# The order of the blocks behind a test at a kernel's end: the general path ahead of the empty arm

## The chip, the core and the metric

The kernel runs on one core of a Trainium2 chip. The metric is device time in microseconds (us): from the start of the program on the core to its end, with all inputs and the output in the chip's memory. The profile shows one execution of the same program, instruction by instruction; its span runs from the first recorded instruction to the last.

## What is computed

The reference is an attention block whose scores are masked by a hash, followed by a Fourier mixing block with a two-layer network. Shapes: batch 4, 8 heads, 768 positions, head size 64, so 512 channels; the hidden layer has 2048 channels.

```python
q_bits = (np.einsum('bhsd,dk->bhsk', q, proj) > 0).astype(np.int64)
k_bits = (np.einsum('bhsd,dk->bhsk', k, proj) > 0).astype(np.int64)
...
mask = q_bucket[:, :, :, None] == k_bucket[:, :, None, :]
scores = scale * np.matmul(q, k.transpose(0, 1, 3, 2))
scores = np.where(mask, scores, -1000000000.0)
scores = scores - np.max(scores, axis=-1, keepdims=True)
attn = np.exp(scores)
attn = attn / (np.sum(attn, axis=-1, keepdims=True) + 1e-09)
...
X = np.fft.fft(x, axis=1)
X = np.fft.fft(X, axis=2)
u = x + np.real(X).astype(np.float32)
un = (u - mean(u)) / np.sqrt(var(u) + 1e-06)
return u + np.maximum(un @ w_ch1, 0.0) @ w_ch2
```

## The kernel before, in words

The program has two complete versions of the computation, one behind the other.

**The main path** (`_main`) is the one that these inputs need. It leaves out the subtraction of the row maximum before the exponential, which is allowed while the scores are small, and it reads the weights from eight-byte words by shifting bits, which is allowed while the weights are ordinary numbers. It works through the four batches: the attention of one batch is interleaved with the mixing and the network of the batch before it. Its last work is the network of batch 3, in `outer7`: PE makes products (L1270), VectorE adds them up with scale (L1282, L1316, L1318, L1322), and SyncE (SP) issues the stores of 128 rows to the output (L1024).

While it works, the main path records the largest norms of queries and keys and whether a weight was out of the ordinary. Before the last batch's network it makes a flag `fl` of these (L1536), and `values_load` (L1539) has every one of the five engines load this flag into a register of its own: the variable `large`.

**The general path** (`_any_scores`, L121 to L483) does everything again without these assumptions. It runs only if the flag is set. With these inputs it is not set, so none of its instructions is executed; but they are in the program of each engine, and they take up room there. In the built program the general path has 260 instructions on SP, 842 on ACT, 1760 on DVE, 116 on POOL and 5288 on PE (matmuls and their weight loads together more).

**The test** is in the last lines of the kernel, L1558:

```python
    with tc.If(large > 0, preferred_fallthrough_block=False):
        _any_scores(tc, *args, cn)
```

An engine has one stream of instructions, laid out block by block. The test becomes, on each engine, a conditional branch (CompareAndBranch) and two arms: the true arm, which is the general path, and a false arm without work. The false arm is not wholly empty. Because the general path would have used up and counted on semaphores, the false arm brings the semaphores to a common state: one wait-and-set on ACT, PE, DVE and POOL, and eight of them on SP, one for each DMA semaphore. SP's waits are for the last transfers of the main path. After the arms comes the end of the program (the profile puts it down to L1589), where all engines meet at a barrier and the semaphores are cleared. On SP the end has 14 semaphore instructions and three drains.

The argument `preferred_fallthrough_block` says which arm lies directly behind the conditional branch and is reached by simply going on. With False, as before, the stream of an engine reads:

```
main path | conditional branch | false arm, jump to the end | general path | end
```

So the kernel before goes on from the branch into the false arm and then jumps over the whole general path to the end. Which queue an instruction stands in isn't touched by any of this: output stores are issued by SP, the five engines each test for themselves, and the order within the main path is fixed ahead of the test.

Of the kernel before, what the change touches and what calls it, by code (L numbers as in the profile page):

```python
# [1552 lines left out]
def kernel(tc, *args):  # L1553

    cn = {n: tc.nc.inline_tensor(a, name="k_" + n) for n, a in _consts().items()}
    with ExitStack() as ctx:
        large = _main(ctx, tc, *args, cn)
    with tc.If(large > 0, preferred_fallthrough_block=False):  # L1558
        _any_scores(tc, *args, cn)


# [32 lines left out]
```

## Time and profile before

| what | value |
|---|---|
| median of 3 runs | 1102.72 us (1101.38 to 1104.4) |
| the profiled execution's own time | 1102.7 us |
| its span, first to last instruction | 1100.4 us |
| granted TensorE clock over the span | 0.994 |
| instructions executed | 14144 |
| VectorE busy | 790.5 us (72%) |
| ScalarE busy | 499.5 us (45%) |
| GpSimd busy | 58.6 us (5%) |
| last matmul group (L1270), start and length | 1085.46 us, 5.34 us |
| last store issued by SP (L1024), start and length | 1092.45 us, 0.90 us |

The span is shorter than the execution's own time by 2.3 us, which lie outside the recorded instructions. Names with a q, such as SPq or DVEq, are the sequencer of an engine: it handles branches, semaphores and the issue of DMAs, and none of this counts as busy time. DMA queues q8 and q14 are of the kind "instruction": what they move are the engines' own instruction streams.

### The profile page before, as it was taken

Reading aid. Unit: us, or ns where it says so; the run is one execution under the profiler, and the core shown is the slowest. Engines: PE = TensorE matmul, PEld = TensorE weight load, DVE = VectorE, ACT = ScalarE, POOL = GpSimd, SP = SyncE. Lnnn points to the kernel's source line nnn. Section 1 sums busy time; section 2 is a strip of 40 time slices with the busy share of each in tenths; the row PEclk is TensorE's granted clock in tenths of the full one; section 3 lists DMA queues with packets and bytes.
Section 4 is the critical chain, followed back from the end, with each engine's and each line's share of the span. In section 5 each row is a group of like instructions: output and inputs, shape, how many; then the busy total and the mean of one; then the engine's idle time right before and its main releaser. Section 6 shows DMA issues by size and latency. Waiting matters only on the chain.

```text
span 1100.4 us, 14144 instructions
## 1 busy us (share of the span) xinstructions
PE 1043.3 (95%) x4933; PEld 632.7 (57%) x4933; DVE 790.5 (72%) x1336; ACT 499.5 (45%) x1055; POOL 58.6 (5%) x132
## 2 busy tenths in 40 slices
PE   7989897999989999999999999999999999999996
PEld 3333353446744675545664576645674569768575
DVE  5899958878599977776767785965856785644353
ACT  6987555553276324454326433355315522340420
POOL 0000000002000020010000011001000002100000
PEclk9999999999999999999999999999999999999998
DMA  9755353451056161322154134213032205122301
GB/s 222 224 95 126 64 140 72 138 164 19 20 149 209 44 204 26 68 63 66 26 157 107 48 82 153 44 43 92 15 129 68 68 24 172 55 81 88 123 20 41
DMA packets 175710, 103.13 MB, mean 94 GB/s; under 512 B 129552, under 2 KB 162960, under 8 KB 175632
## 3 DMA queue, kind: packets, MB, share of 16 engines
q1 hardware_dynamic: 169840, 88.65, 30.1%
q0 software_dynamic: 4224, 13.11, 3.7%
q8 instruction: 41, 0.67, 0.2%
q10 hardware_dynamic: 1568, 0.39, 0.2%
q14 instruction: 37, 0.30, 0.1%
HBM read 81.14 MB, written 20.97 MB: 93 GB/s over the span
## 4 chain that ended last, share of the span: by engine, by line
PE 61%; DVE 11%; ACT 4%; DMA 2%; issue 2%; DVEq 0%; SPq 0%; ACTq 0%
PE o L1270 22%; PE h_p L1390 20%; PE oo L914 6%; PE sc L893 6%; DVE pk L903 3%; PE cs L1086 2%; DMA zraw<-in_moe_w_ch_dram 2%; PE A L1115 2%; PE B L1115 1%; DVE acc L988 1%; ACT rr L948 1%; DVE w L1282 1%; DVE h L1256 1%; PE bits L825 1%; PE un L1141 1%
## 5 line engine op out<-in xcount | busy, mean ns | idle before, releaser
L1270 PE MATMUL o<-w,h 128*128 128x256 f32 x1152 | 259.4, 382 | 1.2 <-ACT tq L1289 0.7
L1270 PEld LDWEIGHTS o<-w,h 128*128 128x128 f32 x1152 | 216.3, 190 | 43.6 <-issue 4.6
L897 ACT ACTIVATE pk<-sc 128x768 f32<-128x768 f32 x192 | 147.6, 809 | 78.4 <-PE sc L893 60.9
L1390 PE MATMUL h_p<-x,w 128*128 128x384 f32 x448 | 163.5, 495 | 3.2 <-ACT h L1412 1.5
L893 PE MATMUL sc<-qt,kt 64*128 64x384 f32 x768 | 155.7, 508 | 6.0 <-ACT pk L897 5.7
L914 PE MATMUL oo<-pk,vn 128*64 128x385 f32 (+1 forms) x768 | 155.3, 499 | 6.0 <-DVE pk L903 3.0
L903 DVE SCALAR_TENSOR_TENSOR pk<-qb,kb,pk 128x768 f32<-128x768 bf16 x132 | 129.0, 1012 | 30.2 <-ACT pk L897 30.1
L1390 PEld LDWEIGHTS h_p<-x,w 128*128 128x128 f32 x448 | 82.3, 190 | 71.0 <-ACT pk L897 5.4
L988 DVE TENSOR_TENSOR acc<-acc,pk 128x1536 f32<-128x1536 f32 (+1 forms) x72 | 105.7, 1482 | 7.2 <-ACT pk L897 6.7
L1390 PE MATMUL h_p<-w 128*128 128x384 f32 x288 | 105.5, 489 | 2.3 <-ACT w L1427 2.3
L914 PEld LDWEIGHTS oo<-pk,vn 128*64 128x64 f32 x768 | 49.1, 136 | 100.0 <-issue 69.3
L893 PEld LDWEIGHTS sc<-qt,kt 64*128 64x128 f32 x768 | 66.9, 188 | 51.3 <-issue 24.0
L1390 PEld LDWEIGHTS h_p<-w 128*128 128x128 f32 x288 | 53.7, 190 | 41.7 <-ACT w L1427 3.5
L1300 ACT COPY tq<-o 128x256 f32<-128x256 f32 x24 | 8.9, 372 | 105.1 <-PE o L1270 105.1
L1282 DVE SCALAR_TENSOR_TENSOR w<-o,rs,w 128x256 f32<-128x256 f32 x56 | 26.7, 478 | 41.6 <-PE o L1270 41.6
L1270 PE MATMUL o<-w 128*128 128x256 f32 x176 | 42.3, 383 | 1.3 <-DVE w L1282 1.3
L1416 DVE TENSOR_TENSOR h<-h 128x384 f32<-128x384 f32 x32 | 17.8, 556 | 33.1 <-ACT h L1415 33.1
L1289 ACT COPY tq<-o 128x256 f32<-128x256 f32 x24 | 8.9, 371 | 69.3 <-PE o L1270 69.2
L1270 PEld LDWEIGHTS o<-w 128*128 128x128 f32 x176 | 32.8, 190 | 8.8 <-DVE w L1282 2.9
L1423 DVE TENSOR_TENSOR h<-h 128x384 f32<-128x384 f32 x32 | 17.7, 553 | 27.0 <-ACT h L1422 27.0
L1024 POOL DMA_DIRECT2D out_dram<-w x30 | 16.4, 548 | 388.7 <-issue 293.2
L1086 PE MATMUL cs<-ch,z 128*128 128x128 f32 (+3 forms) x192 | 33.2, 324 | 3.0 <-DVE bt L829 1.9
(170 smaller groups left out, 1312.4 us busy)
## 6 DMA issues: line engine op xcount, KB each, us to landing
w<-ad SPq DMA_DIRECT2D x168, 128.0 KB, 2.0
w<-bd SPq DMA_DIRECT2D x42, 512.0 KB, 4.5
zraw<-in_moe_w_ch_dram POOLq DMA_DIRECT2D x16, 512.0 KB, 4.0
bd<-w SPq DMA_DIRECT2D x14, 512.0 KB, 3.9
vn<-in_v_dram SPq DMA_DIRECT2D x32, 192.0 KB, 3.4
qn<-in_q_dram SPq DMA_DIRECT2D x120, 48.0 KB, 2.4
kn<-in_k_dram SPq DMA_DIRECT2D x60, 96.0 KB, 3.4
zraw<-in_moe_w_ch_dram SPq DMA_DIRECT2D x8, 512.0 KB, 5.7
```

The source lines that it names most:

```text
L893: last[0] = nc.tensor.matmul(ps[:, h, 0:HALF], kt[rows, ks], qt[rows, qs], start=kb is not None, stop=True,)
L897: nc.scalar.activation(pk[:, g, :, 0:HALF], ps[:, :, 0:HALF], AF.Exp, scale=SCALE)
L903: nc.vector.scalar_tensor_tensor(w, qb[:, h].rearrange("p (g s) -> p g s", g=2), kb[:, h, c : c + 1], w, op0=ALU.is_equal, op1=ALU.mult,)
L914: nc.tensor.matmul(oos[g][h * D : (h + 1) * D, 0:w], nat["v", n][:, (2 * c + h) * D : (2 * c + h + 1) * D], pk[:, g, h, 0:w], start=(c == ...
L988: nc.vector.tensor_tensor(acc[:, g], (first if c == 1 else acc)[:, g], new[:, g], op=ALU.add,)
L1086: nc.tensor.matmul(ps[:, pc + 2 * lo : pc + 2 * hi - 1 : 2], z[:, cp, pc, par, t * P : (t + 1) * P], ch[:, cp, pc, lo:hi], start=(cp == 0) ...
L1115: nc.tensor.matmul(ps[:, cols], F[:, par, k, t, j * P : (j + 1) * P], sq[:, t, k, cols], start=(t == 0), stop=(t == 1),)
L1270: nc.tensor.matmul(ps, a[:, r], right7[i][:, r], start=start and r == 0, stop=r == HF // 2 - 1, skip_group_check=not start,)
L1282: nc.vector.scalar_tensor_tensor(t[:, cols], src, r, t[:, cols], op0=ALU.mult, op1=ALU.add)
L1390: nc.tensor.matmul(ps, left[:, k], right[i][:, k], start=start and k == 0, stop=k == 1, skip_group_check=not start,)
L1416: nc.vector.tensor_tensor(c21, c12, c21, op=ALU.add)
L1423: nc.vector.tensor_tensor(c22, c21, c22, op=ALU.add)
```

## The change

One argument is turned over. The general path is laid directly behind the conditional branch; the false arm follows it, and the end of the program follows the false arm.

```diff
-    with tc.If(large > 0, preferred_fallthrough_block=False):
+    with tc.If(large > 0, preferred_fallthrough_block=True):
         _any_scores(tc, *args, cn)
```

The stream of an engine now reads:

```
main path | conditional branch | general path, jump to the end | false arm | end
```

The instructions themselves are the same. On each engine the built program has as many as before (SP: 1103 in both), and the end of the program begins at the same place in it. The conditional branch now has the opposite condition: where the flag isn't set, it jumps to the false arm. The listing of the program still has a jump at the end of the false arm, but its target is the next instruction, and in the assembled program it is gone; the jump that is left is the one at the end of the general path. Everything ahead of the branch stands where it stood.

## The prediction

> **What bounds the kernel now.** I read the head of the page first, then the end of the chain of waits and the timeline of the last 15 us, and then, for the two lines that the change concerns, the instructions of L1558 (the test) and L1589 (the end of the program), the waits of SP, and the instruction queue in short windows.
>
> The head of the page says what the kernel as a whole is bound by:
>
> ```profile
> span 1100.4 us, 14144 instructions
> PE 1043.3 (95%) x4933; PEld 632.7 (57%) x4933; DVE 790.5 (72%) x1336; ACT 499.5 (45%) x1055; POOL 58.6 (5%) x132
> ```
>
> PE is busy for 95% of the span. Nothing of that can move: the instructions ahead of the branch are the same at the same places. What the change can touch is only what comes after each engine's branch. The last steps of the timeline (start us, length us, engine, line) show where that begins:
>
> ```profile
> 1085.46 5.34 PE L1270 MATMUL o<-w,h 128*128 128x256 f32 x24
> ...
> 1091.94 0.48 DVE L1282 SCALAR_TENSOR_TENSOR u<-tq,rs,u 128x256 f32<-128x256 f32 x1
> 1092.45 0.90 SPq L1024 DMA_DIRECT2D out_dram<-u  x1
> ```
>
> The computation ends at 1092.4 and the span at 1100.4: 8.0 us are a tail with no arithmetic in it. The instructions of the test, all engines (count, min/median/max ns, first and last start us):
>
> ```profile
> L1558 SPq EVENT_SEMAPHORE  x8: 17/17/17, 1095.5 to 1096.0; - x8
> L1558 POOLq COMPARE_BRANCH  x2: 38/39/40, 961.2 to 961.4; - x2
> L1558 PEldq COMPARE_BRANCH  x2: 95/1754/3413, 1087.4 to 1091.0; - x2
> L1558 ACTq COMPARE_BRANCH  x2: 38/46/53, 1088.0 to 1088.2; - x2
> L1558 DVEq COMPARE_BRANCH  x2: 51/56/60, 1092.6 to 1092.8; - x2
> L1558 SPq COMPARE_BRANCH  x2: 41/47/53, 1093.4 to 1096.1; - x2
> ```
>
> Each engine executes two branches: the test, and the jump from the false arm over the general path to the end (both bear the same name here). The instructions of the end:
>
> ```profile
> L1589 SPq EVENT_SEMAPHORE  x14: 17/28/28, 1098.7 to 1100.3; - x14
> ...
> L1589 POOLq DRAIN  x3: 40/107/5388, 961.8 to 1100.1; - x3
> ...
> L1589 ACTq DRAIN  x2: 8/44/81, 1090.7 to 1099.8; - x2
> L1589 PEldq DRAIN  x2: 8/40/72, 1094.5 to 1099.9; - x2
> L1589 DVEq DRAIN  x2: 10/34/58, 1095.8 to 1099.8; - x2
> ```
>
> The two views together give the price of the jump. From the start of the second branch to the first instruction of the end: SP 1096.1 to 1098.7, 2.6 us; ACT 1088.2 to 1090.7, 2.5; DVE 1092.8 to 1095.8, 3.0; PE 1091.0 to 1094.5, 3.5; POOL 961.4 to 961.8, only 0.4. POOL's general path has 116 instructions, SP's 260 and the others' more. SP is last at the barrier, by 2.9 us, so its path sets the end. Its waits, in the last 10 us:
>
> ```profile
> SPq L1558 <- SPq L1558: 2.0, 1, 2.0
> ```
>
> SP comes out of the test at 1093.45, sits 2.0 us until the last output store has landed (1095.5), passes its eight semaphores in 0.6 us, and only then jumps, for 2.6 us. The wait and the jump stand one behind the other.
>
> [...] 2.5 to 3.5 us on the four engines with a far target, and 0.4 on POOL with a near one. In the window 1096.9:1098, inside SP's jump, the instruction queue shows one fetch and no other transfer:
>
> ```profile
> DMA packets 1, 0.01 MB, mean 7 GB/s; under 512 B 0, under 2 KB 0, under 8 KB 0
> ...
> q14 instruction: 1, 0.01, 2.8%
> ```
>
> [...] the trace has 41 and 53 ns on SP. The branch as such is free; the fetch is what is paid. [...]
>
> **The change part by part.** (1) The jump moves from behind the false arm to ahead of it. Its number stays one per engine and its length too, within the 8 instructions of SP's arm: over the general path. (2) The second branch goes: 41 ns on SP, with its step under 0.1 us. (3) The false arm and the end lie next to each other, in the order in which they are executed, with no jump between them.
>
> For SP: the conditional branch starts at 1093.4, as before, since it follows the issue of the last store. It is now the far jump. With SP's own 2.6 us it reaches the false arm at 1093.4 + 2.6 = 1096.0. The last store has landed at 1095.5, so the first semaphore is there already: the 2.0 us wait lies wholly beside the jump. Eight semaphores at the same 0.6 us: 1096.6, and the end begins there instead of at 1098.7: 2.1 us saved. The jump's price is the unknown term. Before, SP's fetch ran on an empty chip (above); after, it runs at about 1094.3, beside the last store. The nearest row for that is DVE's jump, whose fetch fell into the window 1093.5:1094.5 among 150 packets of the store:
>
> ```profile
> q1 hardware_dynamic: 150, 0.14, 40.9%
> q14 instruction: 1, 0.01, 3.9%
> ```
>
> It cost 3.0 us. With this, SP reaches the arm at 1096.4, the end at 1097.0, and 1.7 us are saved. Bounds: with PE's 3.5 us the end begins at 1093.4 + 3.5 + 0.6 = 1097.5, 1.2 us saved. With POOL's 0.4 us the landing at 1095.5 is what SP waits for, and the end begins at 1096.1, 2.6 us saved. More than that isn't there to be had, because the landing and the eight semaphores stay. I take 1.8 us, nearer to DVE's case than to the empty one, because the store is sure to be under way.
>
> The other engines: PE's branch is executed at 1087.4, while its matmuls are queued and run until 1090.8; a jump of 3.5 us ends at 1090.9, and PE is at the barrier some 3.4 us earlier, for no gain. It hides under the last matmuls; without that cover it would end where it did. ACT's ends at 1088.0 + 2.5 = 1090.5. DVE's branch at 1092.6 with 3.0 us ends at 1095.6, 0.2 earlier than before. POOL was through at 961.8 but for a drain of its own. So all four still wait for SP, and SP's gain reaches the end in full. From the first instruction of the end to the last of the span are 1.7 us, as before: the same instructions at the same place.
>
> Sum, against the profiled execution: 1100.4 - 1.8 = 1098.6 us of span, and 1102.7 - 1.8 = 1100.9 us of time, with the 2.3 us outside the span as they were. The median of the runs shown, 1102.72, is the profiled execution's time, so nothing is added.
>
> **The rivals.** *The fetch waits behind the store.* [...] If it is served only after the landing at 1095.5, then SP goes on about 1.7 us after that (in its jump before, the fetch was seen from 1096.9 on and SP went on at 1098.7, at most 1.8): 1097.3, plus 0.6, 1097.9, and 0.8 us are saved: 1101.9. For it: two of the last three stores take about 3 us to land. Against it: DVE's fetch got through in the midst of such packets and delayed DVE by 0.5 us against ACT's empty case.
>
> *A second miss: slower.* If the false arm lies on another page than the end, SP jumps into the first and must fetch the second right after it. That puts a second stall of 2.6 to 3.0 us behind the arm: 1096.0 + 0.6 + 2.6 = 1099.2, or 1096.4 + 0.6 + 3.0 = 1100.0, against 1098.7: 0.5 to 1.3 us slower, 1103.2 to 1104.0. It becomes slower than before as soon as the extra stall is over the 1.8 us gained. For it: a fetch in q14 is 8 KB (37 packets, 0.30 MB on the page of the profile[...])[...]. Against it: the end itself, which is at the same place, ran before without a gap (14 semaphores from 1098.7 to 1100.3)[...]. To be slower by over 3.3 us it would have to stall twice more.
>
> *It does nothing.* If another engine came last, or if SP's store and not its jump set the end, the time would stay at 1102.7. That SP comes to the end 2.9 us after DVE speaks against the first, and the second is the upper bound above, where the gain is largest, not nothing.
>
> **How the numbers follow.** The forecast (1.2 to 2.6 us saved) has 0.77, the waiting fetch 0.10, nothing 0.05, the second miss or a stall that the trace doesn't show 0.08. A difference of under 0.3%, which is 3.3 us, is about what a measurement of this kernel can't tell from no change. The forecast, 0.16%, is inside that, and so is its upper bound of 2.6 us (0.24%). The three runs of before lie 3 us apart, so a median may be off by about 1 us: of the forecast's cases I put 0.14 beyond 3.3 us by scatter, and of the others 0.01. So faster 0.15, same 0.79, slower 0.06, the last from the second miss and scatter together. The range is the forecast's 1100.1 to 1101.5 widened by the scatter below, 0.9 us, and above to the cases of no gain with a little scatter: 1099.2 to 1103.0.
>
> **What would show it right or wrong.** In the profile after: one branch per engine in L1558; SP's eight semaphores begin 2.6 to 3.0 us after its branch, at about 1096.0 to 1096.4 where the branch is at 1093.4, and follow each other without waiting; SP's first instruction of the end follows within 0.1 us of the eighth; PE's branch takes about 3.4 us under its last matmuls; the wait of SP's L1558 on itself is gone or a long pause without a releaser. The prediction is wrong if SP's semaphores start only 3.5 us or more after the branch (the fetch waits), if a gap of over 1 us stands between the arm and the end (a second miss), or if anything ahead of the branch takes another time.

## The result and the profile after

The changed kernel took 1098.18 us (median of 7 runs, 1096.92 to 1100.02), the kernel before 1102.72 us in the same comparison (7 runs, 1100.77 to 1104.4). The ratio is 0.9964 with a 95% interval of 0.9951 to 0.9976: 4.5 us less, where 1.8 were forecast. Two later comparisons of the same two programs gave 0.9983 and 0.9986. So the first thing to settle is how much of the 4.5 us belongs to the change.

Its profiled execution took 1099.06 us, with a span of 1097.1 us. The head of the page of the changed kernel:

```profile
span 1097.1 us, 14139 instructions
PE 1044.5 (95%) x4933; PEld 633.2 (58%) x4933; DVE 790.7 (72%) x1336; ACT 499.3 (46%) x1055; POOL 58.4 (5%) x132
```

Five instructions fewer: one branch on each engine. The instructions of the test in the changed kernel (count, min/median/max ns, first and last start us):

```profile
L1558 SPq EVENT_SEMAPHORE  x8: 17/17/17, 1094.9 to 1095.4; - x8
...
L1558 PEldq COMPARE_BRANCH  x1: 3362/3362/3362, 1085.9 to 1085.9; - x1
L1558 ACTq COMPARE_BRANCH  x1: 54/54/54, 1086.6 to 1086.6; - x1
L1558 ACTq EVENT_SEMAPHORE  x1: 17/17/17, 1089.1 to 1089.1; - x1
...
L1558 DVEq COMPARE_BRANCH  x1: 72/72/72, 1091.1 to 1091.1; - x1
L1558 SPq COMPARE_BRANCH  x1: 50/50/50, 1092.0 to 1092.0; - x1
L1558 DVEq EVENT_SEMAPHORE  x1: 21/21/21, 1094.6 to 1094.6; - x1
```

and those of the end, of which one line matters:

```profile
L1589 SPq EVENT_SEMAPHORE  x14: 17/28/28, 1095.5 to 1097.1; - x14
```

SP's two lines are one row in time. SP branches at 1092.0 and comes to its false arm at 1094.9: 2.9 us for the far jump, now ahead of the eight semaphores. The eight follow each other without a wait (1094.9 to 1095.4), and the end begins at once, at 1095.5; before, 2.6 us lay between. In SP's waits of the last 9 us its pause of 2.0 us, which stood ahead of the jump, has become the jump itself:

```profile
SPq L1558 <- SPq L1558: 2.9, 1, 2.9
```

The last store, issued at 1091.54, lands 2.9 us later, at 1094.4. SP comes out of its jump 0.5 us after that, so the landing costs it nothing any more. PE's jump takes 3.4 us under its own last matmuls, ACT's and DVE's are over before SP's.

From SP's branch to the end of the span that makes 5.1 us, where the kernel before took 1100.4 - 1093.4 = 7.0: 1.8 us less to within the rounding, which is the forecast's figure. But SP's branch itself comes 1.4 us earlier than in the profiled execution of before, and nothing that was changed lies ahead of it. The timeline shows where these 1.4 us are from. The same group of eight matmuls, 276 us after the start, first in the kernel before and then in the changed one (start us, length us):

```profile
277.58 1.89 PE L1270 MATMUL o<-w,w 128*128 128x256 f32 x8
```

```profile
276.20 1.89 PE L1270 MATMUL o<-w,w 128*128 128x256 f32 x8
```

and the last 24 matmuls of the changed kernel, which started at 1085.46 before:

```profile
1084.02 5.34 PE L1270 MATMUL o<-w,h 128*128 128x256 f32 x24
```

1.38 us at 276 us, 1.44 us at 1084 us: the lead is there after the first quarter and stays as it is. The profiled pair is thus 3.6 us apart (1102.7 - 1099.06) for three reasons: 1.8 us in the tail, 1.4 us in the first 276 us, and 0.4 us outside the span (2.3 before, 1.9 after). The experiments ask which of these come back.

### The profile page after: what moved, and what is told of

The parts are those of the page before. It is cut to its first block, busy times and chain, and to the rows that moved or that the text cites. A ratio compares the mean times of both kernels' runs of the same rounds, so it can differ in the third digit from the quotient of the medians.

```text
span 1097.1 us, 14139 instructions
## 1 busy us (share of the span) xinstructions
PE 1044.5 (95%) x4933; PEld 633.2 (58%) x4933; DVE 790.7 (72%) x1336; ACT 499.3 (46%) x1055; POOL 58.4 (5%) x132
## 4 chain that ended last, share of the span: by engine, by line
PE 61%; DVE 12%; ACT 4%; issue 2%; DMA 2%; DVEq 0%; SPq 0%; ACTq 0%
PE o L1270 23%; PE h_p L1390 19%; PE oo L914 6%; PE sc L893 6%; DVE pk L903 3%; PE cs L1086 2%; PE A L1115 2%; DMA zraw<-in_moe_w_ch_dram 2%; PE B L1115 1%; DVE acc L988 1%; ACT rr L948 1%; DVE w L1282 1%; DVE h L1256 1%; PE bits L825 1%; PE un L1141 1%
```

## The experiments

Theory A: the change is worth its tail, because the fetch that the far jump needs now runs beside the last store; the rest is scatter. Theory B: the order of the blocks also makes the part ahead of the branch faster. Other rivals stand with the runs. Where an edit adds lines, the test's line moves from L1558 to L1561 or L1563, and the end's from L1589 to L1592 or L1594.

### Both kernels again, and the general path cut short

The first two of these four runs change nothing. The other two cut the general path to a few instructions, which makes the jump's target near; what they leave out is not executed with these inputs.

```diff
     const = ctx.enter_context(tc.tile_pool(name="const_g", bufs=1))
+    off = const.tile([P, 2], F32, tag="off", name="g_off")
+    nc.sync.dma_start(off, cn["off"].ap())
+    nc.vector.tensor_scalar(off, off, 1.0, None, op0=ALU.mult)
+    nc.sync.dma_start(out[0, 0:P, 0:2], off)
+    return
```

> The kernel before, once more, for the scatter. Theory A (the gain is the far jump laid beside the last store, 1.8 us in the span, and some 0.4 us outside the span; the rest of the 4.5 us between the medians is scatter of the work ahead of the branch): SP's conditional branch starts anywhere from 1091 to 1095 us, the tail from it to the end of the span is 7.0 us again, 2.3 us lie outside the span, median 1101.5 to 1103. Theory B (the order of the blocks also makes the work ahead of the branch faster by 1.5 to 2.5 us): the branch starts at 1093.4 or later and the ratio to the kernel before is 1.000.

Measured: 1102.39 us (14 runs), ratio to the kernel before 0.9996 (0.9985 to 1.0006). The profiled execution took 1105.43 us, 1.9 of them outside the span. So the 2.3 us of the first profile aren't the old order's: 0.4 of the 3.6 us were scatter. The instructions of SP's test in this run:

```profile
L1558 SPq EVENT_SEMAPHORE  x8: 17/17/17, 1098.5 to 1099.1; - x8
L1558 SPq COMPARE_BRANCH  x2: 41/47/53, 1097.0 to 1099.1; - x2
```

Its span is 1103.5, so the tail from SP's branch is 6.5 us. That was 0.5 less than expected: the last store landed 1.5 us after the branch, not 2.0, mostly because its issue, which the branch follows, took 1.24 us and not 0.90. And the branch stands at 1097.0, outside the 1091 to 1095 that I had allowed for: the same program was 3.6 us later there than in its first profile.

> The changed kernel, once more. Theory A: tail from SP's branch to the end of the span 5.1 us, 1.95 us outside the span, and a median 2.2 us (0.2%) below the kernel before, so 1099.5 to 1100.8. Theory B: a median 4 us or more below (0.36%), at 1098.5 or less, with SP's branch at 1092.0 or earlier.

Measured: 1100.95 us (22 runs), ratio 0.9983 (0.9973 to 0.9993), with 1102.85 for the kernel before beside it: 1.9 us. SP's branch came at 1094.6, later than before's first profile; the tail was 1099.5 - 1094.6 = 4.9 us. The median is 0.15 us above the range that I had given. Theory B wanted a branch at 1092.0 or earlier and 4 us again; neither came.

> Order as before, but the general path is cut to a load, one VectorE operation and a store (it isn't executed with these inputs; the kernel no longer serves inputs that would need it). The jump now has a near target on every engine. Theory A: SP's jump falls from 2.6 us to POOL's 0.4, so the tail from SP's conditional branch to the end of the span is 7.0 - 2.2 = 4.8 us, and the median lies 2.2 to 2.6 us below the kernel before, like the changed kernel's or a little better. Rival C (the jump costs as much whatever its target; the distance is no matter): tail 7.0 us, time as before.

> The same cut, with the changed order. Theory A: SP waits only for the landing of the last store and its eight semaphores, tail 2.1 + 0.6 + 1.7 = 4.4 us, which is 0.4 us less than with the order of before and the same cut: with a near target the order hardly matters. Rival C: the tail is 5.1 us and 1.8 us below the cut kernel in the order of before. Theory B: this order makes the part ahead of the branch faster by 1.5 us or more here too.

Measured: 1098.57 us (0.9964, 0.995 to 0.9978) with the order of before, 1098.82 us (0.9965, 0.9951 to 0.9979) with the changed one. SP's lines of the test, first the order of before, then the changed one:

```profile
L1563 SPq COMPARE_BRANCH  x2: 46/48/49, 1092.3 to 1092.6; - x2
L1563 SPq EVENT_SEMAPHORE  x2: 17/17/17, 1092.4 to 1092.5; - x2
```

```profile
L1563 SPq EVENT_SEMAPHORE  x2: 17/17/17, 1092.8 to 1092.9; - x2
L1563 SPq COMPARE_BRANCH  x1: 50/50/50, 1092.6 to 1092.6; - x1
```

With a near target the second branch of the old order is at 1092.6 and the end begins at 1092.8, 0.2 us later, where the far one took 2.6. The spans are 1095.3 and 1095.6, so both tails are 3.0 us: the order makes no difference once the jump is near. This kills rival C, and it shows that what the change earns is the stall of the far jump and not the branch that is gone. My 4.8 and 4.4 us were too much, for two reasons. The short general path uses few semaphores, so SP's arm has two to pass and not eight, and the wait for the landing moves into the end. And the last store landed 1.7 us after its issue began, where it took 3.0 in the kernel before (the last section comes back to this). With a tail of 3.0 us against the changed kernel's 4.9 in the same comparison, the changed order leaves about 2 us of what the long general path costs.

### A border of a fetch laid into the false arm

The prediction's slower rival was a second miss, between the false arm and the end; a page there is the 8 KB that one fetch in q14 moves. It can be made: 26 small loads more in the general path, which aren't executed, push SP's arm along its stream. One run has the changed order, the other the order of before.

```diff
     nc.sync.dma_start(off, cn["off"].ap())
+    spare = const.tile([P, 2], F32, tag="spare", name="g_spare")
+    for i in range(26):
+        nc.sync.dma_start(spare[i : i + 1], cn["off"].ap()[i : i + 1])
```

> The changed order, with 26 small loads more in the general path (27 instructions of SP with what goes with them; they aren't executed). They push SP's false arm and the end along its stream, so that by my reading of when q14 fetches come (one in 128 instructions of SP) a border of a fetch lies among the eight semaphores of the arm. Theory A with a stall at the border: SP comes to the arm 2.6 us after its branch, passes some of the eight, then stands about 1.9 us until the following page, which is asked for 0.55 us after the jump has ended, is there; tail from SP's branch to the end of the span 5.0 + 1.9 = 6.9 us, so the change's gain is gone and the time is that of the kernel before. Rival D (what follows the target page is there in time): no gap among the semaphores, tail 5.0 us, 2 us faster than before.

Measured: 1102.33 us (14 runs), ratio 1.0 (0.9989 to 1.0011): the gain is gone. SP's lines of the test and of the end in this run:

```profile
L1561 SPq EVENT_SEMAPHORE  x8: 17/17/17, 1093.6 to 1095.9; - x8
...
L1561 SPq COMPARE_BRANCH  x1: 50/50/50, 1090.8 to 1090.8; - x1
```

```profile
L1592 SPq EVENT_SEMAPHORE  x14: 17/28/28, 1096.0 to 1097.6; - x14
```

The eight semaphores take 2.3 us and not 0.5; the trace's single instructions have the fourth at 1093.86 and the fifth at 1095.69, so 1.8 us are lost between these two. The last store's packets had ended by 1091.9. In the window 1093.9:1095.6 of this run nothing moves but one fetch:

```profile
q14 instruction: 1, 0.01, 1.8%
```

It starts at 1094.15, 0.56 us after SP has gone on, and SP stands until 1.5 us after that. The tail is 1097.6 - 1090.8 = 6.8 us, against 6.9 expected. Rival D falls: the transfer of what comes after the target's 8 KB starts only after the jump has ended, 0.56 us after it here. When it was asked for, the trace doesn't show.

> The same 26 loads in the general path, in the order of before: the jump's target, the end, lies behind the border, all of it on one page. Theory A: tail 6.5 to 7.0 us, jump 2.7 us, time as before (ratio 1.000). If it is 2 us slower or more, the padding costs something by itself and the run with the changed order must be read against this one.

Measured: 1101.37 us (14 runs), ratio 0.999 (0.9978 to 1.0002). Its branches and its arm:

```profile
L1561 SPq EVENT_SEMAPHORE  x8: 17/17/17, 1094.0 to 1094.5; - x8
L1561 SPq COMPARE_BRANCH  x2: 41/47/53, 1092.4 to 1094.6; - x2
```

with a span of 1098.9: a tail of 6.5 us, as without the loads. The padding costs the old order nothing, and the new one its whole gain.

### The last stores issued by another engine

If SP waits for its jump and no longer for the store, an earlier branch on SP should help. ACT is idle at the end, so it can issue the last store, and SP's branch follows the store before that.

```diff
-    def store(b, T, src, cols):
+    def store(b, T, src, cols, queue=None):
...
-            (nc.sync if b == B - 1 else nc.gpsimd).dma_start(
+            (queue or (nc.sync if b == B - 1 else nc.gpsimd)).dma_start(
...
-                store(b, j + GT, v, high)
+                store(b, j + GT, v, high, nc.scalar if b == B - 1 and j == GT - 1 else None)
```

> The changed order, and the last store of all (128 rows, high half of the last tile) issued by ACT, which is idle by then, instead of SP. SP's branch no longer follows the last store's issue, but that of the store before it, 0.4 to 1.3 us earlier, and its jump lies beside the landing. Theory A: from the end of the last VectorE add to the end of the span 7.9 us before and 6.2 with the change become 5.0 to 5.5; ACT's own far jump comes after its issue and ends before SP's end sequence does. About 1 us below the changed kernel, 3 us below before (0.9973). Rival E (the jump isn't what SP waits for any more; or ACT's jump, now late, becomes last at the barrier): 6.2 us or more, no gain over the changed kernel.

Measured: 1100.27 us (11 runs), ratio 0.9983 (0.997 to 0.9996), no better than the changed kernel in its later comparisons. From the last VectorE add (1092.95) to the end of the span (1099.05) it is 6.1 us. So E's number came, and the reason is in ACT's lines of the end:

```profile
L1589 ACTq DRAIN  x2: 8/8/8, 1096.9 to 1097.6; - x2
L1589 ACTq EVENT_SEMAPHORE  x2: 17/17/17, 1097.5 to 1099.0; - x2
```

The other engines pass the closing barrier at 1098.1; ACT comes to its last semaphore at 1099.0, 0.9 us after them. ACT was now late enough for a border in its own end to show: a fetch starts at 1097.44, 0.6 us after ACT has come out of its jump, and ACT goes on 1.6 us after that, just as SP did with the loads.

> As the one before, with the last two stores issued by ACT. Theory A: SP's jump is wholly done before the last store lands, and the tail from the last VectorE add is 4.8 to 5.3 us, unless ACT's two issues delay each other (SP's last but one took 1.25 us to issue), which makes ACT's branch and so ACT's arrival at the barrier late: then 5.5 to 6.2 us.

For this run the high half of the tile j goes to ACT as well (`store(b, j, u, high, ...)` with the same queue). Measured: 1100.95 us (22 runs), ratio 0.9986 (0.9977 to 0.9995). The tail is 1101.4 - 1094.9 = 6.5 us, over both of the ranges that I had given: ACT stands in the same way for 1.6 us, one step earlier in its end (barrier passed by SP at 1099.5, by ACT at 1101.1). Taking this off leaves 4.9, by subtraction and not by a run.

The border can be moved away as it was moved in before, with copies on ACT in the general path, which aren't executed:

```diff
     nc.gpsimd.memset(mhalf, -0.5)
+    spare = const.tile([P, 1], F32, tag="spare", name="g_spare")
+    for i in range(40):
+        nc.scalar.copy(spare, mhalf)
```

> The changed order with the last store issued by ACT, and 40 small copies more on ACT in the general path (not executed), which push ACT's arm and end away from the border that made ACT stand 0.93 us inside the closing barrier in the run without them. Theory A: no gap in ACT's end, and the tail from the end of the last VectorE add to the end of the span falls from 6.1 to about 5.2 us, where 7.9 were before: some 2.7 to 3 us below the kernel before, 0.997 to 0.9975, about 1 us below the changed kernel. If the 0.93 us were the barrier's and not a fetch's, the tail stays at 6.1 us.

Measured with one store on ACT: 1100.47 us (22 runs), ratio 0.9977 (0.9969 to 0.9986). ACT's gap is gone, so it was a fetch's. The tail from the last add is 1101.4 - 1095.6 = 5.8 us, and not 5.2: SP's last issue took 1.5 us in this run, so its branch came late. The median is 2.05 us below the kernel before, where I had expected 2.7 to 3.

> The same store on ACT and the same 40 copies, in the order of before. Theory A: SP passes its test earlier but still waits for the landing before it jumps, so its far jump of 2.7 us is as bare as before; the tail from the last VectorE add is 7.4 to 7.9 us and the time that of the kernel before (ratio 0.999 to 1.000). If storing on ACT is what gains, the time falls here as well, by 1 us or more.

Measured in the order of before: 1101.99 us (22 runs), ratio 0.9992 (0.9981 to 1.0002), no gain that can be told from none. SP's lines of the test:

```profile
L1561 SPq EVENT_SEMAPHORE  x8: 17/17/17, 1098.2 to 1098.7; - x8
L1561 SPq COMPARE_BRANCH  x2: 41/47/53, 1094.7 to 1098.7; - x2
```

SP tests at 1094.7, waits for the landing until 1098.2 and jumps then; its end begins 3.1 us after that, and the tail from the last add is 1103.44 - 1095.08 = 8.4 us, 0.5 over the upper end of what I expected. Storing on ACT is worth nothing as long as the jump comes after the wait.

> The changed kernel a third time, since its median lay 4.5 us below the kernel before in its first seven runs and 1.9 us in 22 later ones. If the change is worth its tail (1.7 to 1.8 us) and the rest is scatter of the first 275 us, the ratio is 0.998 to 0.9986 again. If the first result was the true one, it is 0.9964 or less.

Measured for the changed kernel, unaltered: 1101.06 us (16 runs), ratio 0.9986 (0.9974 to 0.9998), 1.5 us between the medians. Its tail from SP's branch is 1102.1 - 1097.1 = 5.0 us.

> The changed order, the last two stores issued by ACT, and 40 small copies more on ACT in the general path, so that no border lies in ACT's end. SP's branch then follows an earlier store and its far jump is done before the last store lands; what SP waits for is the landing, 3.0 us after the start of the last store's issue (by the runs so far), then 0.6 us for the arm and 1.7 us for the end. Theory A: tail from the end of the last VectorE add to the end of the span 5.0 to 5.3 us (7.9 before, 6.2 with the change, 5.8 with one store on ACT and the copies), 0.9970 to 0.9977 of the kernel before. If ACT's own jump becomes last at the barrier, 5.6 us or more.

Measured with two stores on ACT and the copies: 1100.38 us (22 runs), with 1103.49 for the kernel before beside it, ratio 0.9971 (0.9962 to 0.998). The tail from the last add is 1099.94 - 1094.67 = 5.3 us. SP's lines of the test:

```profile
L1561 SPq EVENT_SEMAPHORE  x8: 17/17/17, 1097.7 to 1098.3; - x8
...
L1561 SPq COMPARE_BRANCH  x1: 50/50/50, 1093.8 to 1093.8; - x1
```

The last issue began at 1094.7 on ACT, and SP's first semaphore, 3.0 us later, is again the landing: the jump is out of the way. By its tail this is the best of the versions that keep the general path whole, 0.9 to 1.0 us ahead of the changed kernel (6.1, 6.3 and 6.3 us from the last add in the three profiles of that one); by the times the intervals overlap. Some 0.2 us of its gain in time lie outside the span, where it has 1.8 us in the median of its runs, and the kernel before and the changed one have 1.95.

## Why the prediction was right or wrong

*The jump's place and price: right.* SP's far jump took 2.9, 2.6 and 2.8 us in the three profiles of the changed kernel, inside the 2.6 to 3.0 between which I chose. The tail from SP's branch is 7.0, 6.5 and 6.5 us in three profiles with the order of before (the kernel before twice, and the one with the 26 loads), 5.1, 4.9 and 5.0 with the change: 6.7 - 5.0 = 1.7 us. Counted from the last VectorE add, which leaves SP's issue of the last store inside, the same six profiles have 7.9, 7.8, 7.8 and 6.1, 6.3, 6.3: 1.6 us. Of the signs of being wrong that I had named, one came, a different time ahead of the branch. It came in the repeat of before as well (SP's branch 3.6 us later), so it tells nothing about the change.

*The arm and the end without a gap: right.* 1095.4 to 1095.5. The run with a border in the arm shows that this hung on where a fetch's instructions begin and not on the order alone: 1.8 us were lost there, as much as the change had gained. How many instructions one fetch holds is an estimate from the trace of the kernel before: fetches in q14 stand where SP has executed 81, 210, 338, 466, 592 and 721 instructions (67.1, 237.3, 466.6, 600.8, 769.3 and 972.1 us), 126 to 129 apart, though the trace doesn't say which engine a fetch is for. I had given this rival, together with stalls that the trace doesn't show, 0.08. Its mechanism is real; its stall is smaller than the 2.6 to 3.0 us of my sum.

*The fetch doesn't wait behind the store: right.* In the changed kernel SP's jump of 2.9 us ran while the last store was written, and was 0.3 us longer than the old one, which came after the landing: in the window 1093:1094 q14 moved one packet among 16 of q1, and the store landed at 1094.4. Two slips in my case for this rival changed nothing: all three last stores of before took 2.9 to 3.0 us to land, not two of them, and my 1097.3 goes with a wait of 1.8 us, not with the 1.7 beside it.

*The other engines hide theirs: right.* PE's 3.4 us lay under its matmuls, ACT and DVE came to the end at 1089.2 and 1094.7, SP at 1095.5. I had DVE 0.2 us earlier than before. It came 1.1 us earlier in a profile that leads by 1.4, so 0.3 later: its jump took 3.4 us and not 3.0. It still came 0.8 us before SP. PE's jump is hidden; whether its fetches are is open (last section).

*The sum against the median: wrong.* The step that failed is the term for scatter: "a median may be off by about 1 us", with "so nothing is added" and 0.9 us of room at the lower end of the range. It was read from three runs 3 us apart. Over 45 runs of the changed kernel the single run goes from 1096.92 to 1104.8, and the mean of its first seven (1098.4) is 2.6 us below that of the next 22 (1101.0). In the first comparison this scatter put 2.7 us on top of the tail's 1.8. The two later comparisons, with 38 runs of the changed kernel and 90 of before, have means of 1101.25 and 1102.90 us: 1.65 us, what the tail says.

*Where the scatter lies* is shown; what sets it in a given run, only in part. In the repeat of before the group of eight matmuls at 277.58 comes at

```profile
280.81 1.89 PE L1270 MATMUL o<-w,w 128*128 128x256 f32 x8
```

3.2 us late, and the last 24 matmuls are 3.2 us late as well (1088.69 against 1085.46). From 280 us on, all fourteen profiles run in step to within half a microsecond. In the first 280 us the granted TensorE clock isn't always full. The windows 15:40 and 120:160 (busy us of PE, PEld, DVE, ACT, POOL with counts, then the granted clock, the DMA share and GB/s), first in the first profile of before and then in its repeat:

```profile
15.00:40.00 25.00, 22.95 (x156) 9.21 (x154) 19.60 (x32) 22.23 (x40) 0.00 (x0) 1.00 0.92 293
120.00:160.00 40.00, 36.67 (x211) 20.32 (x212) 28.02 (x47) 21.58 (x43) 1.32 (x2) 0.96 0.35 88
```

```profile
15.00:40.00 25.00, 22.13 (x136) 9.06 (x137) 19.23 (x31) 19.88 (x35) 0.00 (x0) 0.93 0.89 283
120.00:160.00 40.00, 36.00 (x218) 19.70 (x212) 26.82 (x44) 21.86 (x47) 1.32 (x2) 0.96 0.41 97
```

In 25 us at a mean of 0.93 the repeat has 136 matmuls instead of 156. The clock drops to half for 3.4 us at a time (in two profiles once for 6.8), and the profiles have one to four such spells in the first 280 us, at different places. Since all fourteen have the same 4933 matmuls in the same order, one profile can be laid over another, matmul by matmul. Ten have a spell between 139 and 148 us. The other four (the short general path in the changed order, both runs with the 26 loads, and one store on ACT without copies) each gain 1.6 us on the first profile of before from 130 to 150 us, where none of the nine others shifts by as much as 0.1. So the clock is one cause, at up to 1.6 us a spell; a spell between 112 and 120 us, which six profiles have and that one hasn't, costs 0.2 to 0.7.

Over the 45 runs of the changed kernel, time and mean granted clock go together with a correlation of -0.74, and the first seven had a mean clock of 0.9949 where the next 22 had 0.9938 and the last 16 had 0.9929. The 0.0011 between the first seven and the next 22 are about 1.2 us of full clock over the 1100 us, an estimate, and less than half of the 2.6 us between their means. So there is more than the clock: the changed kernel's first profile has three spells against two in before's and is still 1.4 us ahead at 276 us. Why the first seven runs lie so low together stays open. The two later comparisons ran on chips 3 and 6; on which chip the first ran isn't known, so a difference between chips isn't excluded, though the kernel before ran beside the changed one each time.

## What to carry to other kernels

The far jump over a long block took 2.5 to 3.5 us in the kernel before, with an 8 KB fetch inside SP's, against 0.2 us on SP with the short general path and 0.4 us on POOL; SP's two branches as such took 41 and 53 ns. For a kernel like this one, lay the block that is rarely run so that the far jump stands ahead of a wait that has to be made anyway, such as that for the last store, and not behind it: here that took 1.7 us off the tail. Then see what is late next: with the last store on ACT it was ACT's end that came last, until the copies moved the border. No run here takes the general path, so what the new order costs there isn't shown. A gain of 0.2% needs both the tail of the trace, which repeats to 0.2 us from the last VectorE add and to 0.5 us from SP's branch, and enough runs, since seven of them here were 2.6 us off.

## What the runs showed of the hardware

- After a far jump the transfer of the following 8 KB starts only about 0.6 us after the engine has gone on, and the engine has it 1.5 to 1.6 us later (three profiles: 26 loads in the changed order, one store and two stores on ACT without copies). A border within the first instructions behind the target is a second stall: 1.8 us on SP, 0.9 and 1.6 us on ACT. So instructions that are never executed, 26 loads in the general path, moved the time of the changed kernel by as much as the change did.
- The last store of 128 KB landed 2.8 to 3.0 us after its issue began in nine of the fourteen profiles, with SP and with ACT issuing it (1092.45 to 1095.5 in the kernel before, 1094.7 to 1097.7 with two stores on ACT and the copies). It isn't a constant: 1.7 us in both runs with the short general path, and 1.8 to 2.2 in three others.
- In eight profiles SP's issue of the last store or of the one before it took 0.9 to 1.7 us; all of SP's other issues of the last three stores took 0.33 to 0.5. In the changed kernel's first profile the long one was the last but one:

```profile
1090.20 1.25 SPq L1024 DMA_DIRECT2D out_dram<-w  x1
```

In each of the eight, a 16 KB fetch in q8, the queue in which one follows PE's jump by 1.0 us (at 1091.99 after 1091.0 in the kernel before, at 1086.95 after 1085.9 in the changed one), moves during more than half of the issue (here from 1090.03 to 1091.10). In the two runs with the short general path no such fetch comes in the last 16 us, and the issues take 0.33 to 0.38 us. So it goes with PE's fetching: the one behind PE's jump in the order of before, and the one after it in the changed order, where PE jumps some 3.6 us earlier. A long issue moves SP's branch, and by that the gain of one run. No run moves PE's fetch alone, so that it is the cause isn't shown.
